# Half-empty key blocks of sliding-window attention multiplied as pairs of 128x64 array tiles

## The chip, the core and the metric

The kernel runs on one core of one Trainium2 chip. A core has five engines that run their own instruction streams and meet at semaphores: TensorE (PE, matrix multiply; its weight loads are listed apart as PEld), VectorE (DVE), ScalarE (ACT), GpSimd (POOL) and SyncE (SP, which here only issues DMAs). The metric is the device time of one execution in microseconds, as the median of the runs shown.

## The reference

The input is a sequence of 2048 tokens of 512 features. Four layers follow each other, linear attention (A), sliding-window attention (B), A, B, each on the layer-normalised input, each added to the residual. All have 32 heads of 16 features. Cut to what matters:

```python
def _A_ref(x, wqkv, wo):
    q, k, v = split(x @ wqkv)                       # 32 heads of 16
    phi = lambda t: jnp.where(t > 0, t + 1, jnp.exp(t)) + 1e-6
    pq, pk = phi(q), phi(k)
    kv = jnp.einsum("bhsd,bhse->bhde", pk, v)
    z = jnp.einsum("bhsd->bhd", pk)
    o = jnp.einsum("bhqd,bhde->bhqe", pq, kv) / (jnp.einsum("bhqd,bhd->bhq", pq, z)[..., None] + 1e-6)
    return merge(o) @ wo
...
def _B_ref(x, wqkv, wo):                            # window W = 256
    q, k, v = split(x @ wqkv)
    scores = jnp.einsum("bhqd,bhkd->bhqk", q, k) * (Dh ** -0.5)
    mask = (idx[:, None] - idx[None, :] >= 0) & (idx[:, None] - idx[None, :] < W)
    p = _softmax(jnp.where(mask[None, None], scores, -1e9), axis=-1)
    return merge(jnp.einsum("bhqk,bhkd->bhqd", p, v)) @ wo
...
x = x + _A_ref(_layernorm(x), A_wqkv, A_wo)
x = x + _B_ref(_layernorm(x), B_wqkv, B_wo)
x = x + _A_ref(_layernorm(x), A_wqkv, A_wo)
x = x + _B_ref(_layernorm(x), B_wqkv, B_wo)
```

## The kernel before, in words

The sequence is cut into 16 tiles of 128 tokens. The program runs in stages: the keys of layer 1 (`layer_a_keys`), a barrier in which the sums over all tokens become small matrices (`barrier`), then `middle(2)`, which for each tile ends layer 1, does all of layer 2 and begins layer 3, a second barrier, and `middle(3)`, which ends layer 3 and does layer 4. The two `middle` stages hold the sliding-window attention.

**Sliding window.** Two heads are worked on at once, so there are 16 pairs of heads, numbered by `f` (0 to 3) and `gq` (0 to 3). Keys stand in blocks of 64, and a block of two heads fills 128 partitions. For the key tile `j` (blocks 2j and 2j+1) `b_scores` multiplies the queries of the tiles j and j+1 with the keys in 32x128 array tiles, four `gq` at once (line 638), and ACT takes the exponential from PSUM into the buffer `pb` (line 648; in layer 4 a fourth buffer in `vp`). `b_far` does the same for the last 64 queries that a block reaches (lines 712 and 715, 725). Two triangles have to be cleared: the near one, on the diagonal (`mk`, lines 657 and 658, or 735 in layer 4), and the far one at the window's end (`mf`, lines 743 and 744). A mask is done on POOL by `affine_select` (657, 743) or on DVE by a product with a table of ones and zeros (658, 735, 744); which engine does which one is fixed by a table.

**Values.** `b_values(j, h)` is called for the query tile j and each half h, the pairs of heads with f = 2h and 2h+1. For each pair of heads it multiplies up to six key blocks, 128 probabilities columns of a block as the weights and the 34 value columns of the two heads (16 values and a one for each) as the moving side, into one PSUM bank (line 764). The six blocks of a tile are 2j, 2j-1, 2j-2, 2j-3, all of whose 128 columns matter, and two of which only half matters: of block 2j+1 only the last 64 queries see any key, and of block 2j-4 only the first 64. The other 64 columns of these two are zeros that stand in the buffer. A half thus takes 48 matmuls from the third tile on. Then DVE takes the reciprocal of the sums (`rcp`, line 775) and multiplies (`div`, line 776), a DMA transposes the result, and `b_out` projects it (line 406) and adds the residual (line 574). `b_values_end` does the last tile of layer 4 in another order.

**Order.** No loop order reaches the chip. `Plan` makes a list of operations with what each reads and writes. `place` takes from a packed table (`TABLE`) the place of every operation in one overall order, its engine where it has a choice, and its PSUM bank (8 banks). `synchronise` puts semaphore waits where an operation needs another engine's result. Each engine plays its operations in that order and waits in line: what stands behind a waiting instruction waits too. The costs in `act`, `dve`, `mm` and the like served to make the table and set nothing on the chip. `PAR` likewise.

Of the kernel before, what the change touches and what calls it, by code (L numbers as in the profile page):

```python
# [223 lines left out]
class Plan:  # L224
# [523 lines left out]

    def b_values(self, j, h, key):
        K = self  # L750
        rp = self.rp
        ps = Tile(1, K.cls)
# [3 lines left out]
        for f in (2 * h, 2 * h + 1):  # L756
# [16 lines left out]
        s = j % 2  # L773
        v = lambda: K.ps(ps)[:, 0:272].rearrange("p (u a d) -> p u a d", u=8, a=2)
        self.on("DVE", "rcp", lambda e: e.reciprocal(K.rc[:, s, h, :].rearrange("p (u a) -> p u a", a=2), v()[:, :, :, 16]), key + 0.02, dve(16, "recip"), wr=[("rc", s, h)], ps=[ps])
        self.on("DVE", "div", lambda e: e.tensor_tensor(
            K.o[:, s, :].rearrange("p (a r d) -> p r a d", a=2, d=DH)[:, 8 * h:8 * h + 8],
            v()[:, :, :, 0:16], K.rc[:, s, h, :].rearrange("p (u a) -> p u a", a=2).unsqueeze(3).to_broadcast([P, 8, 2, DH]), ALU.mult),
            key + 0.03, dve(256), rd=[("rc", s, h)], wr=[("o", s, h)], ps=[ps])

    def b_values_end(self, j, h, key):
# [22 lines left out]
        for k in range(2):  # L804
# [13 lines left out]
        s = j % 2  # L818
        v = lambda: K.ps(ps)[:, 0:272].rearrange("p (u a d) -> p u a d", u=8, a=2)
        self.on("DVE", "rcp", lambda e: e.reciprocal(K.rc[:, s, h, :].rearrange("p (u a) -> p u a", a=2), v()[:, :, :, 16]), key + 0.02, dve(16, "recip"), wr=[("rc", s, h)], ps=[ps])  # L820
        self.on("DVE", "div", lambda e: e.tensor_tensor(
            K.o[:, s, :].rearrange("p (a r d) -> p r a d", a=2, d=DH)[:, 8 * h:8 * h + 8],
            v()[:, :, :, 0:16], K.rc[:, s, h, :].rearrange("p (u a) -> p u a", a=2).unsqueeze(3).to_broadcast([P, 8, 2, DH]), ALU.mult),
            key + 0.03, dve(256), rd=[("rc", s, h)], wr=[("o", s, h)], ps=[ps])
# [44 lines left out]
    def middle(self, ph):  # L869
# [37 lines left out]
        for j in range(T):  # L907
# [12 lines left out]
            for h in range(2):  # L920
                (self.b_values_end if last and j == T - 1 else self.b_values)(j, h, base + j + (h + 1) / 2 + par["k_pv"])
# [26 lines left out]
    r"w;>IN#84O-U&1Rm4QcT;yn$122M8Gj73Rep@D}dEOo)f^F&*Z^{1^sj!8=HR=`jN~fWj~YhJr?e1+X9{#6;K-8o_&Tm>9!iI1G<fz+y(s3lT6P=7aoD05V}A",
    r"ER0343}nWl7#Xu*RxAa>ASp(|Bv>7bK}9Hr!=X54$C6kCDq&C<0okwwR>bmH11n%n3<R~X4(5c)SOp70Q*4IKu_{)>6|fRkK?|&njj=TbfwHg~nqW(;i}i2~",
    r"oPqk-5F20{JPVDm6_$W=a2|HSZrB5RVK|P!kvIy6;!K={v+)2P#Cz}oM&lS9i>q)S%)xQE8t39Lybt4X9?r*)Faa;XCs>0Eur0R3LpTK&;scn9YjGN`!x=ac",  # L950
    r"*W+%Sgza%MK7<a~1v}y%ED3vYDK5k1*a<h_BJ7MCaWO8z!&n*uQD6!}kDw}ih9fu~ui;U=j$hy+Uc$>*gl=FU42(r72p+@ZxB@rfJ-m;_Xg>zUV7M8#U}TCy",
    r"`|trqrLMRYA7M8PO2H^N6^CuO9dF_etOh6WBtF5F_!yt!Ej)#%@hYCdvsj!;&~1!HaVP|Zq;q(JPEvHbgYl>&ouar@m8#JdtWGf~7L}sXbQg!wa2i27@id*G",
    r"WH^#y(nCB;u_*y1$M}?pQebxsMWJaIj-t`@9zWnmEJNop3?-zpRE`o;N_>rP@Dq-qBvhV~QBn#^sqihn!*CRy(ozJfMYZW1UBL5HgT_)iN>3T60#&3+)QIX(",
    r"U7AiaXeKqG&-ewu;y3(`K=r65C8vyp)R;0+X39e2s6I8In?&>sFVHQzO<AcSF+IoeG=V143w(vms0B5ri*$)D(@QLcrLhc_#d6q^Qcy}tMcJr5b)b&aiRRE;",
    r"%1%v5NYOm1LTN~op&XQxQd2JKOc7~5Sz17gC=zv{uH<MT<)%Co1*2j#%uC&95>2Khw3s&1CYnOaC_2W#&9sGj;8I#at7tj(#9r7N``}7iP5CH46`)WYn!|8G",
    r"Dny0p5k00W6qdKrHrh_%_!T{&tF(h&Q+cky;W+}op?mazD$_N(PZhZm&!X<sgL+agx=U~ADfOm4)R%H#PHaWFupi~dJb06D@ojERvAGSkrH2%UBXVDyO>wy&",
    r"KBE`Zj;8Qb?oT^u7d@w!G>t3s8d^(LcsK2#z4V#B&@`G#Rk<2}rEj#3)>9Hr%HIhXIT`Px1RRN@G4Te9&M|lZ4WvXoh^BKwPRuFz4n^iDJcDQQEFMhNxi;6~",
    r"8<dKN&`^rXcQ_^A<usg*uTx!4&RKas9iW4BkF#-hPRmVsHZwP4VZ}MPIk)82yp%OB<5nD>4cFjzl%6fu<PQ{&m-8V?%{jRizo$>sf*l9qHk^xda~^KX?YRLr",
    r"<VJj-57QB9$499nf23aAn~%|P>cE}36UX9J+=u(}8qUl4I6trEIUJa~@H&pk{kT6D;DWrK3vpo%!W(!1H{lFCkQ;LmF3QDtEobBvJeN1}AYQ<kI16Xy{y2~4",
    r"^CsTR4|pLj;#d5d>+t{_f)6<;2jeX~5Z`cc9*l!<8*k@$vV-HxR!$%ZB?Rx};#`7Da(ynvr8$vw<-y#Ym+%lC%H4PvCzd4gl%Mf)4#|&r7eD4FJe)`HNZ!p!",  # L960
    r"Wj`O_gZ!EIaARpAhqx#A;1%+f_wguR%<uUNuav{wRGP^uIl|xgC?DewypliicLqU8Cg~-EB$rRzTv|v=*~=_SMsr44Eh1V{NJ<GJK_!c{lB|+VNP<alInF2e",
    r"B#+^-JdSfnE;+@g`3%41?2=P*O9%-m<9PzV<4_V>Qb_?RB&nsKyp?y7M)F8LIm_qxy}aO(Qc7A&ds!oS<vg#Iby8S9$VcfZy(N>BmNL>oUUEliBW<Ofgppp-",
    r"SNcn4xxo3Qtdx_m(oY765htG{oLuBfTwW^3dg&rvCA>tCh+^fle38q1g|G5Z877frr|go6+)XBNAc-u)rHJg7ic(2NNHK{bMJ2FI<_)q%ic24<EL9|(Y?XmB",
    r"NCwL|882yNo9vVQQdK5MCz&WiWTRA*O|n_8@pV2R)#V1)kVA4<qDnM5BGIL@)RgWrNhV7Pi6K)Yrks*9GF84xEIH`?(I$0Tv^pjy#3)uhq?R0&%W_4I%O0^R",
    r"unMYzsIyXA>c~mCE?4E6+>o2HSAwg$QcrG4eVHcHC8U}m-^8iVDukLTv*f#EQlMtbZON>%sIY2|%$0dEQo^VP(oh=7C>bqdB#^ozcjcbkm+)%41XB@IGZjuX",
    r"S1r^*wL>DRb8=n|slzIix*)M-ti+MH5?Mu2^JRf7ltuDD9!ezjNTRBX@<1(?C2~m~su(J!ilrW@+$yh%t>UP->alvFvMZ(XsC+7(dMwdYPIW{bRibjJ`0AKC",
    r"rB18->WnI&&Z=B$sVtM_5?vKkg;h~?PMudpR2fxP6;kb0NA*-aQ`uAp)mpVt<y3jqNflESR9jV1RZ^8z8BU-QszfTWN}`^tcIt)du6n8-Dyb^V<v5vosd}lb",
# [186 lines left out]
```

## Time and profile before

| | before |
|---|---|
| time, median of 3 runs (lowest to highest) | 407.0 us (405.63 to 408.3) |
| span of the profiled execution | 405.4 us, 18074 instructions |
| PE, PEld busy | 386.1 us (95%), 263.9 us (65%) |
| DVE, ACT, POOL busy | 333.6 us (82%), 341.5 us (84%), 149.2 us (37%) |
| granted TensorE clock | 1.000 |

The profiled execution's own time is given by its span alone, from the first to the last instruction: 405.4 us, 1.6 us under the median of the runs and just under the lowest. A busy PE counts each matmul until its result has drained, so matmuls overlap in it: "x48 ... 1.36" is 48 matmuls from the start of the first to the end of the last. In a row such as `L764 PE MATMUL ps<-vB,pb 128*128 128x34` the first pair is the shape of the array tile, rows and columns, and the second the moving operand. Idle time is listed with what ended it; idle time of an engine that nobody waits for costs nothing.

### The profile page before, as it was taken

What the parts mean: (1) busy time and instruction counts of PE and PEld (TensorE: products, weight loads), DVE (VectorE), ACT (ScalarE), POOL (GpSimd) and SP (SyncE); (2) the same over time, 40 slices, a digit from 0 to 9 for tenths busy, and PEclk for the clock granted to TensorE, in tenths of its full rate; (3) what the DMA queues carried; (4) which work ended last, traced back from release to release, by engine and by line L of the source; (5) the groups of instructions that cost most, each with busy time, mean ns of one, the idle gap of its engine ahead of it and who ended that gap; (6) DMA issues with size and microseconds to landing.
All of it is one profiled execution on the core that took longest, in us unless ns stands there. A gap on an engine that the chain in (4) does not pass through costs nothing.

```text
span 405.4 us, 18074 instructions
## 1 busy us (share of the span) xinstructions
PE 386.1 (95%) x7930; PEld 263.9 (65%) x8004; DVE 333.6 (82%) x759; ACT 341.5 (84%) x439; POOL 149.2 (37%) x243
## 2 busy tenths in 40 slices
PE   8999999998999999999999999999999999999896
PEld 3644776766576566666666777677767775566665
DVE  6998898979998798887858789997898759776775
ACT  2655568998999999999998445999999999999994
POOL 3555624534363545541752213141132221232212
PEclk9999999999999999999999999999999999999999
DMA  8734216333253545353232000335224433344443
GB/s 250 243 66 128 82 41 127 106 80 92 71 94 69 122 97 101 63 129 81 62 79 56 20 2 12 96 83 135 69 57 108 110 76 75 82 118 94 115 124 107
DMA packets 67062, 37.75 MB, mean 93 GB/s; under 512 B 47688, under 2 KB 62152, under 8 KB 66984
## 3 DMA queue, kind: packets, MB, share of 16 engines
q1 hardware_dynamic: 66640, 35.67, 36.3%
q8 instruction: 63, 1.03, 1.2%
q0 software_dynamic: 336, 0.92, 0.7%
q14 instruction: 15, 0.12, 0.1%
q10 hardware_dynamic: 8, 0.00, 0.0%
HBM read 6.29 MB, written 2.10 MB: 21 GB/s over the span
## 4 chain that ended last, share of the span: by engine, by line
PE 76%; ACT 16%; DVE 5%; issue 2%; DMA 1%; ACTq 0%
PE ps L406 25%; PE ps L420 19%; PE ps L764 13%; ACT pb L648 10%; PE ps L638 6%; PE ps L481 3%; PE ps L715 2%; ACT pb L725 2%; ACT vp L648 2%; PE ps L712 1%; DMA xT<-xn 1%; PE ps L1067 1%; ACT vp L725 1%; PE ps L457 1%; DVE XQ L563 1%
## 5 line engine op out<-in xcount | busy, mean ns | idle before, releaser
L648 ACT ACTIVATE pb<-ps 128x1024 bf16<-128x1024 f32 (+3 forms) x224 | 198.4, 974 | 7.1 <-PE ps L638 5.5
L764 PEld LDWEIGHTS ps<-vB,pb 128*128 128x128 bf16 x2496 | 75.2, 96 | 10.4 <-issue 3.9
L764 PE MATMUL ps<-vB,pb 128*128 128x34 bf16 x2496 | 80.2, 177 | 0.3 <-DVE pb L744 0.2
L420 PE MATMUL ps<-xT,wBp 128*128 128x128 bf16 x1024 | 68.5, 219 | 0.9 <-DMA xT<-xn 0.6
L420 PEld LDWEIGHTS ps<-xT,wBp 128*128 128x128 bf16 x1024 | 58.8, 98 | 10.9 <-issue 4.5
L429 ACT ACTIVATE tE<-ps 128x512 bf16<-128x512 f32 x64 | 37.6, 605 | 26.3 <-PE ps L406 16.5
L743 POOL TENSOR_SCALAR_AFFINE_SELECT pb<-pb 128x1024 bf16<-128x1024 bf16 x32 | 36.9, 1152 | 53.8 <-DVE pb L735 37.6
L657 POOL TENSOR_SCALAR_AFFINE_SELECT pb<-pb 128x512 bf16<-128x512 bf16 x51 | 34.3, 673 | 48.4 <-ACT pb L648 20.6
L725 ACT ACTIVATE pb<-ps 128x1024 bf16<-128x1024 f32 x50 | 49.3, 1052 | 2.0 <-PE ps L715 1.0
L574 DVE TENSOR_TENSOR xres<-ps,xres 128x512 bf16<-128x512 f32 x63 | 42.9, 682 | 9.4 <-PE ps L406 9.1
L370 POOL TENSOR_TENSOR rs<-ve,negh 128x1 f32<-128x1 f32 x64 | 37.2, 581 | 32.1 <-DVE ve L369 27.5
L638 PE MATMUL ps<-XQ,kB 32*128 32x256 bf16 (+3 forms) x992 | 47.0, 264 | 1.7 <-ACT pb L648 0.5
L406 PE MATMUL ps<-wA,XQ 128*128 128x512 bf16 x179 | 45.7, 379 | 1.8 <-issue 0.8
L367 DVE BATCH_NORM_STATS2 stats<-xres 128x6 f32<-128x512 bf16 x64 | 43.8, 686 | 2.7 <-DMA xres<-in_A_x_dram 1.8
L420 PE MATMUL ps<-XQ,wA 128*128 128x128 bf16 x512 | 35.4, 219 | 0.1
L369 POOL TENSOR_SCALAR ve<-mv 128x1 f32<-128x1 f32 x45 | 11.5, 255 | 64.4 <-DVE mv L368 62.4
L420 PEld LDWEIGHTS ps<-XQ,wA 128*128 128x128 bf16 x512 | 30.6, 98 | 5.5 <-issue 0.7
L406 PE MATMUL ps<-wBv,xT 128*128 128x512 bf16 x108 | 30.1, 380 | 2.9 <-issue 1.4
L638 PEld LDWEIGHTS ps<-XQ,kB 32*128 32x128 bf16 x992 | 14.9, 92 | 26.4 <-ACT pb L648 8.4
L406 PE MATMUL ps<-wBo,oT 128*128 128x512 bf16 x103 | 28.6, 380 | 3.1 <-issue 1.9
L406 PE MATMUL ps<-M,XQ 128*128 128x512 bf16 x114 | 29.7, 380 | 1.3 <-issue 0.6
L406 PEld LDWEIGHTS ps<-wA,XQ 128*128 128x128 bf16 x192 | 17.0, 97 | 19.6 <-issue 2.1
(128 smaller groups left out, 569.1 us busy)
## 6 DMA issues: line engine op xcount, KB each, us to landing
vB<-vS SPq DMA_DIRECT2D x64, 136.0 KB, 2.6
kB<-vp SPq DMA_DIRECT2D x64, 128.0 KB, 2.2
wA<-in_A_wqkv_dram SPq DMA_DIRECT2D x3, 512.0 KB, 5.0
out_dram<-xres SPq DMA_DIRECT2D x9, 128.0 KB, 2.8
xres<-in_A_x_dram SPq DMA_DIRECT2D x2, 512.0 KB, 4.9
pb<-in_B_wqkv_dram SPq DMA_DIRECT2D x1, 1024.0 KB, 5.6
out_dram<-xres POOLq DMA_DIRECT2D x7, 128.0 KB, 2.2
xres<-in_A_x_dram SPq DMA_DIRECT2D x3, 256.0 KB, 4.7
```

Source lines behind the costliest of these rows:

```text
L367: self.on("DVE", "stats", lambda e: e.bn_stats(K.stats[:, t, :], K.xres[:, t, :]), key, dve(512), rd=[("xres", t)], wr=[("stats", t)])
L370: self.pow = self.on("POOL", "pow", lambda e: e.tensor_tensor(K.rs[:, t, :], K.ve[:, t, :], K.negh[:], ALU.pow), key + 0.03, (640, 690), r ...
L406: m = e.matmul(K.ps(ps), lhs(c), rhs(c), start=c == 0, stop=c == 3)
L420: m = e.matmul(K.ps(ps)[:, f * P:(f + 1) * P], w(c, f), xT(c), start=c == 0, stop=c == 3)
L429: self.on("ACT", "E", lambda e: e.activation(K.tE[:, s, :], K.ps(ps), ACT.Exp, bias=0.0), key, act(512), wr=[("tE", s)], ps=[ps])
L574: self.on("DVE", "res", lambda e: e.tensor_tensor(K.xres[:, t, :], K.ps(po), K.xres[:, t, :], ALU.add), key, dve(512), rd=[("xres", t)], w ...
L638: m = e.matmul(K.ps(ps[gq])[:, ns * i:ns * i + ns], K.kB[rows, j % 4, 2 * f + b, :, :], K.XQ[rows, f, q:q + ns], start=True, stop=True, ti ...
L648: return e.activation(out(h, ns).rearrange("p (f g) c -> p f g c", f=n), i, ACT.Exp, bias=0.0, scale=0.25)
L657: return e.affine_select(out=x, in_=x, compare_op=ALU.is_ge, fill=0.0, base=1, pattern=[[0, 4 * n], [2, 64]], channel_multiplier=-1)
L725: return e.activation(o.rearrange("p (f g) b c -> p f g b c", g=2), i, ACT.Exp, bias=0.0, scale=0.25)
L743: return e.affine_select(out=x, in_=x, compare_op=ALU.is_ge, fill=0.0, base=-2, pattern=[[0, 16], [-2, 64]], channel_multiplier=1)
L764: m = e.matmul(K.ps(ps)[:, 34 * u:34 * u + 34], K.P((b // 2) % rp)[:, f, gq % 2 * 2 + gq // 2, o:o + P], K.vB[:, (b // 2) % 4, b % 2, r, : ...
```

## The change

For query tiles from the third on (but not the last of layer 4) `b_values` is replaced by `b_pairs`. It uses one PSUM bank for each half as before, and splits the 96 matmuls of a tile into two kinds of operation. Four operations, one for each `f`, hold the four full key blocks: 16 matmuls each on the whole 128x128 array. Two operations, one for each half, hold the two half-empty blocks: 16 matmuls with 64 weight columns each, those of block 2j-4 in the array's columns 0 to 63 and those of block 2j+1 in columns 64 to 127, one after the other, so that two neighbours work in different tiles of 128x64. They write PSUM partitions 0 to 63 and 64 to 127. The zeros are no longer read. The number of matmuls is the same: 864 of them (54 halves with 16) change from 128 to 64 weight columns. The four full operations no longer wait for the mask of the near triangle of block 2j+1 and that of the far triangle of block 2j-4; the small one does. `rcp` and `div` move into a helper, `divide`, unchanged.

The table is another one: the order, banks and engines of all operations are set anew. Beside the 54 new operations the engine differs for 114 others; in sum 13 masks go from POOL to DVE (7 of 128x1024, line 743 to 744, and 6 of 128x512, line 657 to 658), and some copies from PSUM go from DVE to ACT or back. In the program PE changes the shape of its array tiles 329 times before and 385 times now.

```diff
+    def b_pairs(self, j, key):
+        K = self
+        rp = self.rp
+        banks = [Tile(1, K.cls) for _ in range(2)]
...
+        full = ((2 * j, 0), (2 * j - 1, 64), (2 * j - 2, 128), (2 * j - 3, 192))
+        vals = lambda i: [("vB", i % 4, a, b) for a in range(2) for b in range(2)]
+        for f in range(4):
+            def put(e, f=f):
+                m = None
+                for gq in range(4):
+                    u = 4 * (f % 2) + gq
+                    for b, c in full:
+                        o = 384 * (b % 2) + c
+                        m = e.matmul(K.ps(banks[f // 2])[:, 34 * u:34 * u + 34], prob(b, f, gq)[:, o:o + P], val(b, f, gq), start=f % 2 == 0 and gq == 0 and b == 2 * j, stop=False, skip_group_check=True)
+                return m
+            rd = [("F", (j - 2) % rp, h_) for h_ in (0, 1)] + [("F", (j - 2) % rp, 1, 1)]
+            for i, bs in ((j - 2, (1,)), (j - 1, (0, 1)), (j, (0,))):
+                rd += [("P", i % rp, f)] + vals(i)
+                rd += [("P", i % rp, f, b, h_) for h_ in range(3) for b in bs]
+            self.pe("pv", put, key + 0.5 * (f // 2) - 0.001 * (f % 2), 16, 34, rd=rd, ps=[banks[f // 2]])
+        for h in range(2):
+            fs = (2 * h, 2 * h + 1)
+            def put(e, h=h, fs=fs):
+                m = None
+                for f in fs:
+                    for gq in range(4):
+                        u = 4 * (f % 2) + gq
+                        for half, b in ((0, 2 * j - 4), (1, 2 * j + 1)):
+                            o = 384 if half else 256
+                            m = e.matmul(K.ps(banks[h])[64 * half:64 * half + 64, 34 * u:34 * u + 34], prob(b, f, gq)[:, o:o + 64], val(b, f, gq), start=False, stop=True, tile_position=(0, 64 * half), skip_group_check=True)
+                return m
+            rd = [("F", (j - 2) % rp, h_) for h_ in (0, 1)] + [("F", (j - 2) % rp, 0, 1)] + vals(j - 2) + vals(j)
+            for f in fs:
+                rd += [("P", i % rp, f) for i in (j - 2, j)] + [("P", j % rp, f, 1, h_) for h_ in range(3)]
+            self.pe("pv", put, key + 0.5 * h, 16, 34, mode=(128, 64), occ=256, rd=rd, ps=[banks[h]])
+            self.divide(j, h, key + 0.5 * h, banks[h])
...
-            for h in range(2):
-                (self.b_values_end if last and j == T - 1 else self.b_values)(j, h, base + j + (h + 1) / 2 + par["k_pv"])
+            end = last and j == T - 1
+            if j >= 2 and not end:
+                self.b_pairs(j, base + j + 0.5 + par["k_pv"])
+            else:
+                for h in range(2):
+                    (self.b_values_end if end else self.b_values)(j, h, base + j + (h + 1) / 2 + par["k_pv"])
...
 TABLE = (
-    r"c-qx^1GFSt(r#$0ZQHhO+qP}nwr$(CZQHi_XPvtD&h*^wnSO8n_11b>mANZp2fp|sa-YnqbKl)_58WdNK!9-Dg#d<Npdb_oXow5(AUK4EFc2RSKtf0aiNU}f",
...
+    r"c-qBz1Jor~({Am;#u?kTZQIP)cE*#jZQIV+wrwM0BV+6D^PW4w+)R@1TmQPZ-|pVswRcrL^;C6rpY?`@Xg&gfun-QyLku56NC*WneQ|vWAR$D6L=X`oK~oTj",
...
```

On PE, near the end of layer 2's attention, this stood before (the first two rows are projections of the next layer; 764 the values; 638 the scores; a row's size is that of its output):

```order
L406 MATMUL ps<-wA,XQ 128x512 x4
L420 MATMUL ps<-XQ,wA 128x128 x16
L764 MATMUL ps<-vB,pb 128x34 x48
L638 MATMUL ps<-XQ,kB 128x256 x8
L764 MATMUL ps<-vB,pb 128x34 x48
L638 MATMUL ps<-XQ,kB 128x256 x8
L406 MATMUL ps<-wA,XQ 128x512 x8
L638 MATMUL ps<-XQ,kB 128x256 x8
```

At the same place there now stands (765 are the full key blocks, 783 the pairs, with 64 output partitions each):

```order
L406 MATMUL ps<-wA,XQ 128x512 x4
L420 MATMUL ps<-XQ,wA 128x128 x16
L765 MATMUL ps<-vB,pb 128x34 x32
L783 MATMUL ps<-vB,pb 64x34 x16
L638 MATMUL ps<-XQ,kB 128x256 x8
L765 MATMUL ps<-vB,pb 128x34 x32
L783 MATMUL ps<-vB,pb 64x34 x16
L638 MATMUL ps<-XQ,kB 128x256 x8
L406 MATMUL ps<-wA,XQ 128x512 x8
L638 MATMUL ps<-XQ,kB 128x256 x8
```

Nothing else moved here: each 48 became 32 and 16, and between the full blocks and the scores there is one more change of the array's shape.

On DVE, in the middle of layer 2, these rows stood from one residual sum (574) to the next; 367, 368 and 371 belong to a layer norm, 395 and 592 are copies from PSUM, 430 and 431 the feature map of layer 3, 658 a mask:

```order
L574 TENSOR_TENSOR xres<-ps,xres 128x512
L367 BN_STATS stats<-xres 128x6
L368 BN_AGGR mv<-stats 128x2
L371 TENSOR_SCALAR xn<-xres,mv,rs 128x512
L430 TENSOR_SCALAR tE<-tE 128x512
L431 SCALAR_TENSOR_TENSOR vp<-ps,tE 128x512
L395 CAST vS<-ps 128x32x16 x2
L658 TENSOR_TENSOR pb<-pb,tri 128x8x64
L371 TENSOR_SCALAR xn<-xres,mv,rs 128x512
L395 CAST vp<-ps 128x512
L658 TENSOR_TENSOR pb<-pb,tri 128x8x64
L574 TENSOR_TENSOR xres<-ps,xres 128x512
```

The same stretch now, with two of the large masks (744):

```order
L574 TENSOR_TENSOR xres<-ps,xres 128x512
L367 BN_STATS stats<-xres 128x6
L744 TENSOR_TENSOR pb<-pb,tri 128x16x64
L368 BN_AGGR mv<-stats 128x2
L430 TENSOR_SCALAR tE<-tE 128x512
L395 CAST vS<-ps 128x32x16
L431 SCALAR_TENSOR_TENSOR vp<-ps,tE 128x512
L395 CAST vp<-ps 128x512
L395 CAST vS<-ps 128x32x16
L371 TENSOR_SCALAR xn<-xres,mv,rs 128x512
L574 TENSOR_TENSOR xres<-ps,xres 128x512
L744 TENSOR_TENSOR pb<-pb,tri 128x16x64
```

Both far masks of one key tile, done on POOL before, have come into DVE's line, ahead of a copy that frees a PSUM bank; the near masks have gone to other places.

More of the change, by code (lines that the diff above doesn't have):

```diff
@@ L772, in b_values @@
             self.pe("pv", put, key - 0.001 * (f % 2), 4 * len(blocks), 34, rd=rd, ps=[ps])
[L773 to L779, printed above, removed]
+        self.divide(j, h, key, ps)
     def b_values_end(self, j, h, key):
@@ L817, in b_values_end @@
             self.pe("pv", put, key - 0.001 * (1 - k), 8, 34, rd=rd, ps=[ps])
[L818 to L824, printed above, removed]
+        self.divide(j, h, key, ps)
     def b_out(self, j, key, by_pe):
@@ L948 @@
[L948 to L967, printed above, removed]
```

98 lines of the change are left out of this document (65 added, 33 removed).

## The prediction, made before the changed kernel was run

> **What bounds the kernel now.** I read the page first, then the stages of the sliding window by stretches, then single places in PE's timeline. The page's busy times and its chain of waits:
>
> ```profile
> PE 386.1 (95%) x7930; PEld 263.9 (65%) x8004; DVE 333.6 (82%) x759; ACT 341.5 (84%) x439; POOL 149.2 (37%) x243
> ...
> PE 76%; ACT 16%; DVE 5%; issue 2%; DMA 1%; ACTq 0%
> PE ps L406 25%; PE ps L420 19%; PE ps L764 13%; ACT pb L648 10%; PE ps L638 6%; PE ps L481 3%; PE ps L715 2%; ACT pb L725 2%; ACT vp L648 2%; PE ps L712 1%; DMA xT<-xn 1%; PE ps L1067 1%; ACT vp L725 1%; PE ps L457 1%; DVE XQ L563 1%
> ```
>
> PE carries three quarters of the chain, the value matmuls (764) 13% of it, some 53 us. But ACT carries 16%. The busy times by stretch (columns: time, then PE, PEld, DVE, ACT, POOL, each with its count, clock, DMA share, GB/s), first the two sliding-window stages as a whole, then a stretch in each:
>
> ```profile
> 70.00:220.00 150.00, 143.92 (x3038) 96.84 (x3069) 126.53 (x283) 145.10 (x170) 69.45 (x105) 1.00 0.39 88
> 270.00:395.00 125.00, 118.45 (x3201) 85.02 (x3220) 96.94 (x223) 119.64 (x147) 32.55 (x39) 1.00 0.40 97
> ```
> ```profile
> 120.00:140.00 20.00, 18.39 (x422) 12.42 (x423) 16.17 (x39) 20.00 (x24) 9.61 (x16) 1.00 0.48 88
> 360.00:380.00 20.00, 18.66 (x527) 13.51 (x527) 13.25 (x33) 19.85 (x25) 5.55 (x8) 1.00 0.43 98
> ```
>
> Just where the change acts, ACT is busy 145.1 of 150 us and 119.6 of 125 us, without a pause in some stretches. PE and ACT are both nearly full there; over the 275 us ACT has 4.9 + 5.4 = 10.3 us to spare, and no shortening of PE can bring more than that.
>
> **What it removes.** PE's timeline near the end of layer 2's attention, the place whose order is shown above (start, length from first start to last end, then the instructions):
>
> ```profile
> 197.63 1.06 PE L420 MATMUL ps<-XQ,wA 128*128 128x128 bf16 x16
> 198.53 1.36 PE L764 MATMUL ps<-vB,pb 128*128 128x34 bf16 x48
> 199.82 0.40 PE L638 MATMUL ps<-XQ,kB 32*128 32x256 bf16 x8
> 200.15 1.36 PE L764 MATMUL ps<-vB,pb 128*128 128x34 bf16 x48
> ...
> 206.15 1.36 PE L764 MATMUL ps<-vB,pb 128*128 128x34 bf16 x48
> 207.44 0.34 PE L638 MATMUL ps<-XQ,kB 32*128 32x192 bf16 x8
> 207.72 1.07 PE L420 MATMUL ps<-XQ,wA 128*128 128x128 bf16 x16
> ```
> ```profile
> L764 PE MATMUL ps<-vB,pb 128*128 128x34 bf16 x2496 | 80.2, 177 | 0.3 <-DVE pb L744 0.2
> ```
>
> One value matmul lasts 0.177 us, 48 take 1.36: (1.36 - 0.177) / 47 = 0.025 us from start to start, for 34 columns. The 16 that become pairs are 16 x 0.025 = 0.40 us in each half.
>
> **What a pair costs.** The trace has no 128x64 tile. The nearest rows are the sums' 128x32 tiles (543), four side by side over the same 128 rows, and the far scores of layer 4 (715), 32x64 tiles, eight at once, two of them over the same rows:
>
> ```profile
> 44.80 0.40 PE L543 MATMUL ps<-XQ,zs 128*32 128x128 bf16 x16
> ```
> ```profile
> L543 PE MATMUL ps<-XQ,zs x128: 219/219/219, 44.8 to 306.2; 128*32 128x128 bf16 x128
> ```
> ```profile
> L715 PE MATMUL ps<-XQ,kB x896: 184/209/212, 259.7 to 382.3; 32*64 32x64 bf16 x180
> ```
> ```profile
> 365.49 0.33 PE L715 MATMUL ps<-XQ,kB 32*64 32x64 bf16 x32
> ```
> ```profile
> 365.49 0.71 PE L715 MATMUL ps<-XQ,kB 32*64 32x64 bf16 x64
> 366.13 1.07 PE L420 MATMUL ps<-xT,wBp 128*128 128x128 bf16 x16
> ```
>
> At 543, 16 matmuls have 0.40 - 0.22 = 0.18 us between first and last start: four rounds of four, three steps of 0.06. One 128-column matmul on the whole array takes as much ((1.06 - 0.22) / 15 = 0.056 in the first row above). So tiles beside each other, over the same rows, run at once. At 715 the first 32 start within 0.33 - 0.19 = 0.14 us, four rounds of eight in 0.035 each. In such a round every row of the array takes in two times 64 weight columns and two times 64 moving columns; a 128x64 pair takes in two times 64 and two times 34. So I expect no more than 0.035 a pair, and hardly less than the 0.025 of a single value matmul: eight rounds are 0.20 to 0.28 us. I take 0.25, near the 715 rows. The far ends: (0.71 - 0.21) / 63 = 0.008 a matmul over all 64, so 16 x 0.008 = 0.13 if only issue counts; and eight rounds of 8 x 0.008 = 0.064, 0.51, if the average round of 715 is what counts.
>
> [...]
>
> So PE saves 54 halves x (0.40 - 0.25) = 8.1 us (10.8 at 0.20, 6.5 at 0.28).
>
> **What it adds: changes of shape.** In the rows above, 48 value matmuls fill 48 x 0.025 = 1.21 us, but the scores start 1.29 after them: 0.08 for the change. Back: from 199.82 to 200.15 is 0.33. Eight score matmuls of 256 columns last 0.06 longer than eight of 192 (0.40 against 0.34), so two rounds of 256 stream for about 0.24, and 0.09 is left; at 207.44 it is 0.28 - 0.18 = 0.10. From 715 back to 420 the last start is at 365.49 + 0.71 - 0.21 = 365.99 and the next at 366.13, 0.14, of which 0.03 is its own. I take 0.09 (0.08 to 0.10). The order has 385 changes for 329: 56 x 0.09 = 5.0 us (4.5 to 5.6). PE's sum is 8.1 - 5.0 = 3.1 us less (0.9 to 6.3).
>
> **What it moves.** Masks and copies:
>
> ```profile
> L743 POOL TENSOR_SCALAR_AFFINE_SELECT pb<-pb 128x1024 bf16<-128x1024 bf16 x32 | 36.9, 1152 | 53.8 <-DVE pb L735 37.6 <-ACT pb L725 5.8 <-DVE vp L735 4.3
> L744 DVE TENSOR_TENSOR pb<-pb,tri 128x1024 bf16<-128x1024 bf16 x18 | 12.8, 713 | 0.1
> L658 DVE TENSOR_TENSOR pb<-pb,tri 128x512 bf16<-128x512 bf16 x17 | 7.6, 455 | 1.9 <-ACT pb L648 1.9
> L395 DVE CAST vS<-ps 128x512 bf16<-128x512 f32 x24 | 16.4, 688 | 3.8 <-PE ps L406 3.0 <-issue 0.8
> L395 ACT ACTIVATE XQ<-ps 128x512 bf16<-128x512 f32 x10 | 6.0, 604 | 1.0 <-PE ps L420 0.7
> ```
>
> DVE gets 7 x 0.713 + 6 x 0.455 = 7.7 us of masks and loses about one copy (net, 0.7): 7 us, on 126.5 of 150 and 96.9 of 125 us busy. That lies beside PE and ACT; if the cover went, it would cost all 7. A large mask is ready 0.44 us after its start sooner than on POOL. ACT keeps about its load in these stages (three copies of `bqe` go, three of `bve` and one of `bke` come, at 0.6 to 0.7 us); its other additions are clears in the first 60 us. At the start SP now issues the first `wA` load sixth instead of third, behind `x`:
>
> ```profile
> 1.72 0.50 SPq L286 DMA_DIRECT2D wA<-in_A_wqkv_dram  x1
> ...
> 8.27 1.89 PE L406 MATMUL ps<-wA,XQ 128*128 128x512 bf16 x8
> ```
> ```profile
> wA<-in_A_wqkv_dram SPq DMA_DIRECT2D x3, 512.0 KB, 5.0
> ```
>
> Three places of 0.5 us later it is issued at 3.2 and lands at 8.2, when the first product with it starts today: nothing, or half a microsecond.
>
> What the values wait for:
>
> ```profile
>   POOL pb L657: 1.0, 3
>   ACT pb L648: 0.9, 4
>   DVE pb L658: 0.8, 3
>   DVE pb L744: 0.7, 2
> ```
>
> Masks stop 764 for 1.0 + 0.8 + 0.7 = 2.5 us. Two of the four masks now bind only the small operation, so I count 1.0 us of this as gained, between 0 (it waits in turn, with the scores behind it in PE's line) and 2.5.
>
> **The rivals.** *A, the sum holds:* PE's 3.1 us count by its share of the chain, 76%, 2.4 us, plus 1.0. The span becomes 402.0. By the ends (0.9 and no wait, 6.3 and 1.0) it is 399.6 to 404.7.
>
> *B, the pairs do not pair:* each of the two tiles waits for the other's load, the small operation takes 16 x 0.025 = 0.40 us to 0.51, and the changes of shape are paid on top: 5.0 to 54 x 0.11 + 5.0 = 10.9 us, 76% of it 4 to 8 slower. It decides from a round of (0.40 - 5.0 / 54) / 8 = 0.038 us on, only just above my 0.035. Against it: 543 and the first rounds of 715. For it: 715's average of 0.064. [...]
>
> *C, ACT takes over:* with ACT at 97% and 96%, a PE that is 1% shorter only waits for PSUM banks. Nothing is gained, 405 to 407. The two full stretches are for it, the 10.3 us to spare against.
>
> *D, the new order as a whole is better:* PE stands still 150 - 143.9 + 125 - 118.5 = 12.6 us in the two stages. If half of it goes with the earlier full blocks and quicker masks, 6.3 + 2.4 = 8.7 us less, 398.
>
> *E, DVE's line is late:* all 7 us of it on the path and nothing gained: 414.
>
> **How the numbers follow.** The median of the runs is 1.6 us above this span, so A gives 402.0 + 1.6 = 403.6 (401.2 to 406.3). A measurement of this kernel tells 1%, 4.1 us, from no change. Chances: A 0.42, of which 0.16 under 402.9; B 0.13 (411 to 415); C 0.18; D 0.21 (396 to 401); E 0.06. Faster 0.16 + 0.21 = 0.37, within 1% 0.26 + 0.18 = 0.44, slower 0.19. The range from 396.5 to 411.5 leaves out most of B and E and the lowest of D.
>
> **What would show it.** The pair rows (783): 16 matmuls of 128x64 from first start to last end 0.25 + 0.18 = 0.43 us or less; over 0.58 is B. The start of what follows a pair, 0.08 to 0.10 after its last round, shows the change of shape. PE's busy time should fall by 3 to 8 us; if ACT's share of the two stages rises above 98%, it is C. Reciprocals (now 795) that wait for DVE's own masks would be E. The prediction fails if the rounds of 715 that I read come from instructions queued ahead and a pair behind 32 full matmuls finds none.

## The result, and the profile after

The changed kernel is slower: 411.4 us median of 6 runs (410.3 to 412.9) against 407.2 of 6 of before in the same measurement (405.6 to 408.3), a ratio of 1.0107 with an interval of 1.0080 to 1.0133. The profiled execution has a span of 410.1 us, 4.7 above before's 405.4.

The page's busy times and chain of waits, of after:

```profile
PE 383.8 (94%) x7928; PEld 259.3 (63%) x8004; DVE 337.2 (82%) x775; ACT 345.7 (84%) x442; POOL 136.1 (33%) x226
...
PE 68%; ACT 12%; DVE 10%; issue 4%; DMA 4%; POOL 1%; SPq 1%; POOLq 0%
```

PE's busy time fell by 2.3 us, and yet PE's share of the chain went from 76% to 68%: what grew are DVE (5% to 10%), DMA (1% to 4%) and issue (2% to 4%). The pairs themselves are just what was forecast. PE's timeline in layer 2 of after, at the same kind of place as shown of before:

```profile
209.53 0.96 PE L765 MATMUL ps<-vB,pb 128*128 128x34 bf16 x32
210.42 0.43 PE L783 MATMUL ps<-vB,pb 128*64 128x34 bf16 x16
210.78 0.34 PE L638 MATMUL ps<-XQ,kB 32*128 32x192 bf16 x8
211.06 1.07 PE L420 MATMUL ps<-XQ,wA 128*128 128x128 bf16 x16
```
```profile
L783 PE MATMUL ps<-vB,pb x768: 177/183/204, 94.6 to 400.7; 128*64 128x34 bf16 x192
```

From first to last start the 16 matmuls take 0.43 - 0.183 = 0.25 us, eight rounds of 0.031. The last of the 32 full matmuls starts at 209.53 + 0.96 - 0.177 = 210.31 and fills 0.025, so 0.08 is the change of shape; behind the pairs it is 210.78 - (210.42 + 0.25 + 0.03) = 0.08 again.

Where the time is lost is seen from when each stage's work starts first and last on PE. First the rows of before that the prediction does not show (the last start of layer 2's far scores, 712; first and last start of the scores, 638), then those of after, with the first barrier (543) and layer 4's far scores (715):

```profile
L712 PE MATMUL ps<-XQ,kB x448: 188/188/198, 86.0 to 217.2; 32*128 32x64 bf16 x150
L638 PE MATMUL ps<-XQ,kB x992: 188/265/278, 61.4 to 392.6; 32*128 32x256 bf16 x96, 32*128 32x224 bf16 x89, 32*128 32x192 bf16 x7, 32*128 32x128 bf16 x4
```
```profile
L543 PE MATMUL ps<-XQ,zs x128: 219/219/219, 48.2 to 308.7; 128*32 128x128 bf16 x128
L712 PE MATMUL ps<-XQ,kB x448: 185/188/198, 88.8 to 220.6; 32*128 32x64 bf16 x150
L715 PE MATMUL ps<-XQ,kB x896: 184/209/212, 263.0 to 385.8; 32*64 32x64 bf16 x180
L638 PE MATMUL ps<-XQ,kB x992: 188/265/278, 64.8 to 396.6; 32*128 32x256 bf16 x96, 32*128 32x224 bf16 x89, 32*128 32x192 bf16 x7, 32*128 32x128 bf16 x4
```

The first barrier starts at 48.2 instead of 44.8: 3.4 us are lost in a stage that has not one pair. From there the distance hardly moves: 3.4 at the first scores (64.8 against 61.4), 3.4 at the end of layer 2 (220.6 against 217.2), 3.5 at the last far scores of layer 4 (385.8 against 382.3). So up to there the two sliding-window layers, where all the pairs are, neither gained nor lost. The last scores are 4.0 late, and the end 4.7. Distances of half a microsecond mean little here: the kernel with pairs alone has the order of before up to the barrier, and its barrier starts at 44.3.

The first 45 us, by stretches (columns as before: PE, PEld, DVE, ACT, POOL), of before:

```profile
0.00:20.00 20.00, 18.65 (x135) 10.61 (x138) 15.44 (x44) 9.18 (x15) 9.10 (x26) 1.00 0.79 248
20.00:45.00 25.00, 24.84 (x218) 13.04 (x217) 22.31 (x56) 11.73 (x20) 14.79 (x32) 1.00 0.43 113
```

and of after:

```profile
0.00:20.00 20.00, 16.66 (x117) 8.69 (x119) 14.99 (x45) 8.33 (x15) 8.33 (x23) 1.00 0.77 236
20.00:45.00 25.00, 23.00 (x140) 11.68 (x142) 21.29 (x56) 12.33 (x19) 11.79 (x27) 1.00 0.60 123
```

PE, nearly full there before, is busy 2.0 + 1.8 us less in the same 45 us. SP's timeline of after (283 are loads of `x`, 286 and 291 of weights, 377 transposes), with DVE's first statistics and PE's first product:

```profile
0.80 2.43 SPq L283 DMA_DIRECT2D xres<-in_A_x_dram  x5
3.27 1.02 SPq L286 DMA_DIRECT2D wA<-in_A_wqkv_dram  x2
3.90 0.69 DVE L367 BATCH_NORM_STATS2 stats<-xres 128x6 f32<-128x512 bf16 x1 [2.71 <-DMA xres<-in_A_x_dram]
4.33 6.70 SPq L283 DMA_DIRECT2D xres<-in_A_x_dram  x2
8.70 0.59 PE L406 MATMUL ps<-wA,XQ 128*128 128x512 bf16 x2
11.08 0.51 SPq L286 DMA_DIRECT2D wA<-in_A_wqkv_dram  x1
13.04 1.29 SPq L377 DMA_TRANSPOSE XQ<-vp  x1
15.90 0.37 SPq L291 DMA_DIRECT2D wBo<-in_B_wo_dram  x1
16.32 0.51 SPq L286 DMA_DIRECT2D pb<-in_B_wqkv_dram  x1
20.06 5.18 SPq L377 DMA_TRANSPOSE XQ<-vp  x4
```

and of before:

```profile
2.86 1.46 DVE L367 BATCH_NORM_STATS2 stats<-xres 128x6 f32<-128x512 bf16 x2 [1.66 <-DMA xres<-in_A_x_dram]
7.50 0.37 SPq L286 DMA_DIRECT2D wA<-in_A_wqkv_dram  x1
11.27 0.37 SPq L286 DMA_DIRECT2D pb<-in_B_wqkv_dram  x1
16.37 6.01 SPq L377 DMA_TRANSPOSE XQ<-vp  x4
```

What SP waits for in the first 48 us, in after and in before:

```profile
SPq L283 <- DMA wA<-in_A_wqkv_dram: 5.7, 1, 5.7
```
```profile
SPq L283 <- DMA wA<-in_A_wqkv_dram: 1.1, 1, 1.1
```

With five loads of `x` issued at once, that of the tiles 2 and 3 ahead of that of the first tile, DVE starts at 3.90 instead of 2.86. The kernel's own rule for its loads (line 295) does the rest: from the eighth load of its list on, each waits until the load four places ahead in that list has landed. The last load of `x` therefore waits for the second `wA` load. That one is issued seventh now instead of sixth, and the waiting load stands ahead of the third `wA` load instead of behind it. SP stands for 5.7 us instead of 1.1, until 11.0, and the third `wA` load leaves at 11.08 instead of 7.50. The row of four transposes starts at 20.06 instead of 16.37.

### The profile page after: what moved, and what is told of

Same layout as the page of the kernel before. It is cut to its first block, busy times and chain, and to the rows that moved or that the text cites. A ratio compares the mean times of both kernels' runs of the same rounds, so it can differ in the third digit from the quotient of the medians.

```text
span 410.1 us, 18057 instructions
## 1 busy us (share of the span) xinstructions
PE 383.8 (94%) x7928; PEld 259.3 (63%) x8004; DVE 337.2 (82%) x775; ACT 345.7 (84%) x442; POOL 136.1 (33%) x226
## 4 chain that ended last, share of the span: by engine, by line
PE 68%; ACT 12%; DVE 10%; issue 4%; DMA 4%; POOL 1%; SPq 1%; POOLq 0%
PE ps L406 23%; PE ps L420 17%; PE ps L765 8%; PE ps L638 7%; ACT pb L648 6%; PE ps L783 4%; ACT pb L725 2%; DMA xres<-in_A_x_dram 2%; PE ps L481 2%; PE ps L715 2%; ACT vp L648 1%; DVE vp L431 1%; PE ps L712 1%; DVE stats L367 1%; DMA xT<-xn 1%
## 5 line engine op out<-in xcount | busy, mean ns | idle before, releaser
L429 ACT ACTIVATE tE<-ps 128x512 bf16<-128x512 f32 x64 | 38.2, 610 | 26.6 <-PE ps L406 20.4
L743 POOL TENSOR_SCALAR_AFFINE_SELECT pb<-pb 128x1024 bf16<-128x1024 bf16 x28 | 32.7, 1167 | 68.2 <-DVE pb L735 38.0
L765 PEld LDWEIGHTS ps<-vB,pb 128*128 128x128 bf16 x1536 | 48.2, 96 | 7.9 <-issue 2.6
L765 PE MATMUL ps<-vB,pb 128*128 128x34 bf16 x1536 | 52.1, 177 | 0.0
L406 PE MATMUL ps<-wA,XQ 128*128 128x512 bf16 x181 | 47.3, 379 | 3.8 <-DMA XQ<-vp 1.2
L657 POOL TENSOR_SCALAR_AFFINE_SELECT pb<-pb 128x512 bf16<-128x512 bf16 x45 | 30.8, 683 | 50.3 <-ACT pb L648 22.4
L638 PEld LDWEIGHTS ps<-XQ,kB 32*128 32x128 bf16 x992 | 15.0, 92 | 27.9 <-ACT pb L648 10.4
L795 DVE RECIPROCAL rc<-ps 128x16 f32<-128x16 f32 x64 | 16.3, 255 | 18.1 <-PE ps L783 15.7
```

Of the source, the lines that this page charges most:

```text
L406: m = e.matmul(K.ps(ps), lhs(c), rhs(c), start=c == 0, stop=c == 3)
L429: self.on("ACT", "E", lambda e: e.activation(K.tE[:, s, :], K.ps(ps), ACT.Exp, bias=0.0), key, act(512), wr=[("tE", s)], ps=[ps])
L638: m = e.matmul(K.ps(ps[gq])[:, ns * i:ns * i + ns], K.kB[rows, j % 4, 2 * f + b, :, :], K.XQ[rows, f, q:q + ns], start=True, stop=True, ti ...
L657: return e.affine_select(out=x, in_=x, compare_op=ALU.is_ge, fill=0.0, base=1, pattern=[[0, 4 * n], [2, 64]], channel_multiplier=-1)
L743: return e.affine_select(out=x, in_=x, compare_op=ALU.is_ge, fill=0.0, base=-2, pattern=[[0, 16], [-2, 64]], channel_multiplier=1)
L765: m = e.matmul(K.ps(banks[f // 2])[:, 34 * u:34 * u + 34], prob(b, f, gq)[:, o:o + P], val(b, f, gq), start=f % 2 == 0 and gq == 0 and b = ...
```

## The experiments

### The start, the order behind it, and the pairs

The change has three parts that can be exchanged: the first stage up to the barrier, the order (with engines and banks) behind it, and the pairs. Five kernels have them in other combinations.

Pairs alone, in the order of before:

```diff
-TABLE: order, engines and banks of the changed kernel
+TABLE: those of before; behind the full blocks of each half its 16 pairs
```

> Before's order, engines and banks; only the 54 value halves become 32 whole-array matmuls with the pair operation right behind. Theory 1 (the pairs do what PE's sum said, and the loss is from the new first stage): PE has about 3 us less to do, the time falls by 2 to 3 us, to about 404.5. Theory 2 (ACT or the banks set the pace of the two sliding-window stages, so a shorter PE only waits): within 0.5 us of before. Theory 3 (the changes of shape cost more than the pairs bring): 1 to 4 us slower than before.

408.9 us against 408.2, ratio 1.0008 (0.9985 to 1.0032). The pairs bring nothing that can be told from zero in the order of before; the interval leaves room for 0.6 us. There they need 397 changes of shape, so PE's own sum is 8.1 - 68 x 0.09 = 2.0 us less.

The new order without pairs:

```diff
-o = 384 if half else 256
-m = e.matmul(K.ps(banks[h])[64 * half:64 * half + 64, 34 * u:34 * u + 34], prob(b, f, gq)[:, o:o + 64], val(b, f, gq), start=False, stop=True, tile_position=(0, 64 * half), skip_group_check=True)
+o = 320 if half else 256
+m = e.matmul(K.ps(banks[h])[:, 34 * u:34 * u + 34], prob(b, f, gq)[:, o:o + P], val(b, f, gq), start=False, stop=half == 1, skip_group_check=True)
```

> The changed kernel with its order, engines and banks, but the half-empty blocks are again multiplied whole, with their zeros, on the 128x128 array; no 128x64 tile is left. Theory 1: PE has 3 us more than in the changed kernel, 413 to 414. Theory 2: as the changed kernel, 411 to 412. Theory 3: faster than the changed kernel, 408 to 410.

415.5 us, ratio 1.0156 (1.0118 to 1.0194), slower than any of the three theories had it.

The first stage exchanged, both ways (the first `den` is the barrier's first operation):

```diff
-TABLE: one kernel's order throughout
+TABLE: the other kernel's order, engines and banks up to the first den; its own behind
```

> The changed kernel with the order, engines and banks of before up to the first sums of the first barrier (the instructions on line 543), the loads from HBM included; from there on its own. Theory 1: the 3.4 us that the profile shows lost by then come back, 408.0. If the later stages take the gain up again (they wait for something that is not shifted with the start): 410 to 411.5.

> The kernel before with the first stage of the changed kernel (order, engines, banks up to the first barrier's sums) and its own order behind. Theory 1: 3.4 us slower, 410.5. If the loss at the start is made up later: 407 to 408.

The changed kernel with before's start takes 409.3 us, ratio 1.0018 (0.9995 to 1.0041); before with the new start 410.7, ratio 1.0070 (1.0042 to 1.0098). Last, before's start with the new order behind it, and no pairs:

> The changed kernel's order, banks and engines with the first stage of before, and the half-empty blocks multiplied whole, so without pairs. With the new first stage it was 1.0156. If start and pairs add up (0.9% and 0.5%): ratio 1.005 to 1.009, 409.5 to 411.5, and the order behind the start is itself 0.7% worse than before's. If the new order behind the start is as good as before's and the pairs bring nothing: 0.999 to 1.003. Below 0.998 the new order would be better and the pairs a loss.

410.5 us, ratio 1.0065 (1.0042 to 1.0088). All together:

| start | order behind it | half-empty blocks | ratio to before |
|---|---|---|---|
| before | before | pairs | 1.0008 |
| new | before | whole | 1.0070 |
| before | new | whole | 1.0065 |
| before | new | pairs | 1.0018 |
| new | new | whole | 1.0156 |
| new | new | pairs (the change) | 1.0107 |

The start costs 0.7 to 0.9% in each of the three lines where it can be compared (1.0070; 1.0156 against 1.0065; 1.0107 against 1.0018), 2.9 to 3.7 us. The new order behind it costs 0.65%, 2.6 us, by itself. The pairs bring 0.47% and 0.49% in the new order, 1.9 to 2.0 us (each with some 0.35 to 0.45% of uncertainty), and nothing in the old one. Taken in this sequence, order 2.6, start 3.7, pairs -2.0, the three make up the 4.3 us of the result, as they must: each is the difference of two lines of the table. What is found apart from that is that the start costs much the same in three lines, and the pairs in two.

### The loads at the start

```diff
-SP: x, x, x, x, x, wA, wA, x, x, wA
+SP: x, x, wA, x, x, wA, x, x, wA, x   (all ahead of the rest)
```

> The changed kernel; only the ten loads of x and of layer 1's weights on SP's queue stand in the order of before, ahead of all else. If the order of the loads makes the loss at the start: 3 us faster than the changed kernel, 408 to 409. If it is the order of the work on DVE, POOL and PE behind them: 410.5 to 412.

411.6 us against 408.8, ratio 1.0073 (1.0048 to 1.0098), where the changed kernel has 1.0107: a third of its loss, 1.4 us, though the two intervals overlap. Its microseconds lie in the second of the two ranges set ahead, but beside a before of 408.8; by its ratio it lies between the two. In the trace the first barrier starts at 46.2, between 44.8 and 48.2:

```profile
L543 PE MATMUL ps<-XQ,zs x128: 219/219/219, 46.2 to 307.1; 128*32 128x128 bf16 x128
```

So by this trace 2.0 of the 3.4 us are the order of the ten loads (1.4 by the runs), and the rest is that of the work behind them. The row of transposes belongs to the rest: with before's loads it still starts at 19.32.

### Whether PE or ACT sets the pace

The pairs save PE's time, yet bring nothing in the order of before. Four kernels take much from PE, from ACT, or from both, by leaving out parts of the computation. From ACT, the exponentials of the last 64 queries of most key tiles:

```diff
-i = span(ps[2 * h:2 * h + 2], lambda x: [[ns, n], x, [1, ns]])
+w = ns - 64 if j >= self.rp and ns > 160 else ns
+i = span(ps[2 * h:2 * h + 2], lambda x: [[ns, n], x, [1, w]])
```

and from PE, the half-empty key blocks:

```diff
+if j >= 2:
+    blocks = [(b, c) for b, c in blocks if b not in (2 * j + 1, 2 * j - 4)]
```

> The kernel before, but from the fourth key tile on (the fifth in layer 4) the exponential leaves out the last 64 of the 256 (224) queries that a block of scores holds; what the buffer held before stands there, so some probabilities are old. About 190 exponentials get 0.21 us shorter, 40 us off ACT. Theory 2 (ACT sets the pace of the two sliding-window stages): 8 us faster or more, until PE is the bound. If PE sets it: under 4 us faster.

> The kernel with the pairs alone in before's order, with the same part of the exponentials left out. Theory 2: with ACT out of the way the pairs now bring their 2 to 3 us against the same kernel without pairs. If the pairs bring nothing by themselves (their result is later, the masks hold them up): within 1 us of it.

> The kernel before without the two half-empty key blocks from the third tile on: 16 of 48 matmuls of a half are left out, with no change of shape, so 54 x 0.40 = 21.6 us are taken off PE (the result lacks these keys). If PE's time counts by its share of the chain, 76%: 391. Theory 2: a third of it or less, 400 or slower.

> Leaves out two parts of the computation: the two half-empty key blocks of each query tile (21.6 us off PE) and the exponentials of the last 64 queries of most key tiles (some 40 us off ACT). Alone the first was worth 2.9 us and the second 2.0. If PE and ACT hold each other (each nearly full, so that taking work from one leaves the other), both at once are worth far more than the 5 us of their sum: 12 us or more, 396 or less, ratio under 0.97. If instead a third thing sets the pace (DVE, transfers, the granted clock, the order itself), it stays at about the sum: 402 to 405, ratio 0.985 to 0.992. In the stretch 70:220 PE would be under 142 of 150 us in the second case and the stage would end more than 5 us sooner in the first.

All beside 408.8 us of before, the last beside 407.9:

| | us | ratio to before |
|---|---|---|
| exponentials cut (ACT's busy time falls by 31 us, not the 40 expected) | 406.5 | 0.9950 (0.9925 to 0.9974) |
| the same, with pairs | 405.3 | 0.9913 (0.9884 to 0.9942) |
| half-empty blocks dropped (PE: 864 matmuls x 0.025 = 21.6 us) | 405.6 | 0.9928 (0.9897 to 0.9958) |
| both dropped | 395.6 | 0.9688 (0.9647 to 0.9730) |

21.6 us off PE are worth 2.9 us, 31 off ACT 2.0, and both at once 12.7. By the marks set ahead, the first alone would have named ACT as the bound and the second alone PE. Neither is the bound by itself. That each holds the other is read from the chains and from one group of waits. The chain of waits with the half-empty blocks dropped, with the exponentials cut, and with both:

```profile
PE 53%; ACT 32%; DVE 9%; DMA 3%; issue 1%; SPq 0%; ACTq 0%
```
```profile
PE 88%; DVE 8%; ACT 2%; issue 1%; DMA 1%; POOL 0%; SPq 0%; ACTq 0%
```
```profile
PE 56%; DVE 22%; ACT 13%; DMA 5%; issue 3%; POOL 0%; DVEq 0%; POOLq 0%
```

With less on PE the chain passes to ACT (16% to 32%), with less on ACT to PE (76% to 88%), and with less on both to DVE (22%). The place of it is the scores. Their groups on PE (the last number is PE's idle time before them), of before and with the half-empty blocks dropped:

```profile
L638 PE MATMUL ps<-XQ,kB 32*128 32x256 bf16 (+3 forms) x992 | 47.0, 264 | 1.7 <-ACT pb L648 0.5
```
```profile
L638 PE MATMUL ps<-XQ,kB 32*128 32x256 bf16 (+3 forms) x992 | 47.4, 265 | 11.5 <-ACT pb L648 6.2
```

The scores need PSUM banks that ACT's exponential has to free. PE came there sooner and waited 11.5 us, 6.2 of it for that exponential, instead of 1.7. That the scores are the place is read from these rows; it was not tried apart. A part of what the dropped blocks save is lost to the clock: in 5 of its 8 runs the mean granted clock was 0.996 or less; its three others took 404.5 us in the mean, before's 17 of 24 at a higher clock 407.9, so that some 3.5 us are gained there (see the last section). The pairs, worth 2.0 us of PE's time in this order, gain 406.5 - 405.3 = 1.2 us where ACT has room, and nothing where it has not; the first of these differences (0.37% of ratio) is about as large as its own uncertainty.

### The last tiles

In the trace of the kernel with pairs alone, PE was 1.5 us ahead at the end of layer 2 (the last far scores at 215.7 instead of 217.2) and 1.5 behind at the last scores (394.1 instead of 392.6). Of the 1.5 ahead, 0.5 stood already at the first barrier, ahead of any pair.

```diff
-if j >= 2 and not end:
+if j >= 2 and not (last and j > 11):
```

> Pairs in the order, banks and engines of before, but the last three tiles with pairs in layer 4 keep their half-empty blocks whole: 48 pairs instead of 54. Pairs everywhere in this order gave 1.0008, up to 1.46 us ahead of before at the end of layer 2 and 1.5 behind at the end of the run, where PE waited and its granted clock then fell for 3.4 us. If that place is what loses the gain, this one keeps it: 405.5 to 407.5 against 408 of before, ratio 0.994 to 0.998, and no stretch of lower clock near 387. If the gain goes wherever PE is shortened beside a full ACT, it is 0.998 to 1.002 again.

408.3 us against 407.9, ratio 1.0006 (0.9981 to 1.0032): the last tiles are not what takes the gain away.

### Work moved between ACT, DVE and POOL

If a full ACT holds the pairs back, copies can be taken from it, onto a DVE that is 82% busy. And the masks that the change moves between POOL and DVE, which the prediction counted at nothing, can be exchanged by themselves.

```diff
-engine of 19 copies (10 in the second): ACT
+engine of these copies: DVE, at the same places in the order
```

> Pairs in the order and banks of before, and all 19 copies of queries, keys and values that ACT makes from the first scores on go to DVE instead, at their old places in the order: some 12 us off ACT (0.60 to 0.71 us each), some 13 us onto DVE (0.69 each). Nothing of the computation is left out. If PE and ACT hold each other and DVE has room (126 of 150 and 97 of 125 us busy), a third of what 40 us off ACT gave appears: 404.5 to 407 against 408 of before, ratio 0.992 to 0.998, ACT in 70:220 under 139 of 150 us. If DVE's line becomes the late one, as its place in the order is that of an ACT copy, the copies arrive late and PE waits: 409 to 414, ratio 1.003 to 1.015, with idle time of PE ended by DVE's copies.

> The same with every second one of these copies, 10 of 19: some 6 us off ACT, 7 us onto DVE. If PE and ACT hold each other and DVE has room, half of the gain of all 19: 406 to 408, ratio 0.995 to 1.0. If DVE's line is the late one: 408.5 to 411, ratio 1.001 to 1.008, and less than with all 19.

With 19 copies moved, 416.9 us against 407.2, ratio 1.0252 (1.0224 to 1.0281); with 10 of them 414.4, ratio 1.0182 (1.0153 to 1.0211). Both are beyond what was expected even of a late DVE: with some 12 us moved off a full ACT the kernel is 2.4% slower than with pairs alone. ACT's exponentials with pairs alone, and with all copies moved, in the stretch from 70 to 395 us:

```profile
L648 ACT ACTIVATE pb<-ps 128x1024 bf16<-128x1024 f32 (+2 forms) x216 | 191.4, 974 | 8.0 <-PE ps L638 6.7
```
```profile
L648 ACT ACTIVATE pb<-ps 128x1024 bf16<-128x1024 f32 (+3 forms) x208 | 185.3, 975 | 17.5 <-PE ps L638 16.2
```

ACT now waits 16.2 us for scores instead of 6.7, and the scores wait for DVE; the three longest waits of PE ahead of scores there are all on DVE, where with pairs alone one of 0.4 us was on DVE:

```profile
PE ps L638 <- DVE XQ L563: 1.7, 1, 1.7
PE ps L638 <- DVE vS L395: 1.0, 1, 1.0
PE ps L638 <- DVE XQ L395: 0.9, 1, 0.9
```

```diff
-engine of 51 masks: as in the kernel's own table
+engine of these masks: as in the other kernel (32 POOL to DVE and 19 DVE to POOL, or the reverse), same places
```

> Before, with every mask on the engine that the changed kernel uses for it, at its old place in the order: 32 masks go from POOL to DVE, 19 from DVE to POOL, 13 net as in the forecast. No other part of the change. If masks lie beside other work, as the forecast has it: 407 to 408.5, ratio 0.998 to 1.003. If DVE's line is one of those that hold the pace, as the 12 us of copies put on it showed (10 us slower), the 7.7 us of masks cost 3 to 8 us: 410 to 415, ratio 1.007 to 1.02.

> The changed kernel with the first stage of before (alone 1.0018), and behind it every mask on before's engine, at its new place in the order. If the new order was made for its own engines, this is slower: 410 to 414, ratio 1.004 to 1.015. If DVE's added masks cost time in the changed kernel too, it is faster than before: 404 to 407, ratio 0.99 to 0.998.

Before with the new masks takes 422.8 us against 407.4, ratio 1.0379 (1.0345 to 1.0412); the changed kernel with before's start and masks 418.9, ratio 1.0280 (1.0239 to 1.0320). Exchanged either way it costs 2.6 to 3.8%, more than was expected. In the second a part is the clock's: the mean granted clock was 0.986 to 0.992 in all six runs, and at the 0.990 of the trace that is an estimated 4 us of the 11.5 (1% of its 417.9). In the first, the last far scores of layer 2 start at 227.9 instead of 217.2. The longest waits of the values on PE, in the stretch from 70 to 250 us, are three for masks on POOL; the first two, at 181.2 and 219.7, are for masks that went there from DVE:

```profile
PE ps L764 <- POOL pb L657: 3.8, 3, 1.5
```

They are 2.7 of the 10.7 us; the rest was not followed. The exchange also sets other waits anew, as `place` lets the larger operations of POOL wait for the last large operation of DVE ahead of them, the masks among these. So this does not price the 13 masks of the change. It shows that an engine's choice belongs to its place in the order, and that neither can be costed alone.

## Why the prediction was wrong, point by point

**The pairs and the changes of shape: right.** 0.25 us for eight rounds and 0.08 for a change were measured where 0.25 and 0.09 were taken. Rival B, the pairs that don't pair, is out: a round takes 0.031, under its 0.038. A load of 64 columns lasts 0.113 us here (783), a matmul 0.183, and a round of two of each takes 0.031, so loads and matmuls of the two tiles overlap, though they share all rows. That each tile waits for the other's load, as B has it, is not what the trace shows of this tile. In the new order the pairs bring 55 changes of shape more than whole blocks do (385 against 330), so PE's sum of 3.1 us less stands. The sign that was set for it did not quite come: PE's busy time fell by 2.3 us, not by 3 to 8.

**PE counted by its 76% of the chain: right in size once, wrong as a rule.** 2.4 us were forecast; in the new order the pairs bring 1.9 to 2.0, in the old one nothing. So the near agreement is luck. A share of the chain is not an exchange rate: 21.6 us off PE brought 2.9 (13%), and once ACT was relieved too, 0.9688 instead of 0.9950, 10.7 us (half of it). Rival C, that ACT takes over, fits the old order with pairs, where nothing was gained, but it is not what decided the changed kernel.

**The mask waits, 1.0 us: not there to be gained.** The four waits that the prediction lists stand in an answer that takes PE's weight loads and matmuls together. Nearly all of them are the loads', which run ahead:

```profile
L764 PEld LDWEIGHTS ps<-vB,pb 128*128 128x128 bf16 x2496 | 75.2, 96 | 10.4 <-issue 3.9 <-POOL pb L657 1.0 <-ACT pb L648 0.9
```

The matmuls themselves waited for a mask once, for 0.2 us, as the prediction's own row of 764 on PE says (0.3 in all).

**The start: the first step that failed.** "Nothing, or half a microsecond" was worked out from the one `wA` load and the first product, and that product did come 0.4 us late (8.70 instead of 8.27). But what was moved were ten loads, and each tile's statistics, transposes and products come behind them in a stage where PE was full (43.5 of 45 us); it cost 2.9 to 3.7 us by the runs and 3.4 by the trace. The rest of SP's queue, in which a load of `x` now waits 5.7 us for a `wA` load, ahead of the third one, was not followed.

**The order as a whole: the second.** The sum had no term for it. Rival D gave it a gain of up to 6.3 us, and no rival gave it a loss of its own; E put a loss on DVE's masks alone. Measured without pairs and with before's start, it costs 0.65%, 2.6 us. D's 12.6 us in which PE stands still were also read too high: before's trace lacks 74 matmul records (7930 against 8004 weight loads), and 4.1 of the 12.6 are idle time that ended on no wait ("issue"), of which the trace of the changed kernel with before's loads, with all 8004 records, has none. What the order's loss consists of is not settled. In the trace of the kernel with before's start, the new order and no pairs (408.4, 3.0 over before) the barrier starts at 44.3, the last far scores of layer 2 at 217.6 and those of layer 4 at 383.8, where before has 44.8, 217.2 and 382.3: half of the loss comes behind the last far scores. DVE's two kinds of masks in after are

```profile
L744 DVE TENSOR_TENSOR pb<-pb,tri 128x1024 bf16<-128x1024 bf16 x22 | 14.9, 679 | 0.3 <-ACT pb L725 0.3
L658 DVE TENSOR_TENSOR pb<-pb,tri 128x512 bf16<-128x512 bf16 x23 | 9.8, 433 | 3.4 <-ACT pb L648 3.4
```

14.9 + 9.8 = 24.7 us where before had 12.8 + 7.6 = 20.4 (three more of the 13 stand in another buffer), and DVE's whole busy time grew by 3.6 us, not 7: half of E's 7 us were not there to be late. E's own sign, reciprocals that wait for DVE's masks, did not show: they wait for PE's pairs, 15.7 us, as they did for the values before, 15.9.

**The stages.** ACT is busy 144.6 and 120.3 us in the two stretches (145.1 and 119.6 before), so the mark set for C, above 98%, was not reached:

```profile
70.00:220.00 150.00, 142.37 (x2994) 94.26 (x3024) 126.88 (x286) 144.61 (x168) 64.57 (x98) 1.00 0.40 89
270.00:395.00 125.00, 117.27 (x3161) 83.16 (x3182) 98.78 (x229) 120.28 (x148) 28.51 (x38) 1.00 0.40 95
```

Of the forecast 403.6, then, -2.4 for the pairs held within half a microsecond in this order, -1.0 for the masks had no ground, and +3.7 for the start and +2.6 for the order were missing.

## What to carry to other kernels

When a change comes with a new order of everything, compare the stages that it does not aim at first: the first operation behind each stage, before and after, gives the loss of each in one row. Where two engines are both 95% full and free buffers for each other, as here, time taken from one was worth a small part of itself (2.9 of 21.6 us on PE, 2.0 of 31 on ACT), and only time taken from both brought more than the sum of these (12.7 us). A wait of a weight load is not a wait of PE: read it in the row of the matmuls (those of 764 in before stood idle for 0.3 us, its loads for 10.4). An engine's choice in an order laid out by hand or by search has no price of its own: moved at its old place, work that looks hidden can cost as much as it takes, or more. Here 10 copies, an expected 7 us for DVE, cost some 7, and the new masks in the order of before, by the forecast 7.7 us net for DVE, cost 15.4.

## What the runs showed of the hardware

The granted clock fell by half within a kernel whose PE was 82% busy in the 6 us ahead. In the kernel with half-empty blocks dropped, by stretches, 366 to 372 us and the 3.41 us behind it:

```profile
366.00:372.00 6.00, 4.95 (x163) 3.35 (x162) 4.26 (x10) 6.00 (x8) 1.25 (x2) 1.00 0.20 70
372.10:375.51 3.41, 3.41 (x40) 2.86 (x38) 1.51 (x3) 2.20 (x3) 0.43 (x1) 0.50 0.65 142
```
```profile
371.71 3.28 PE L420 MATMUL ps<-xT,wBp 128*128 128x128 bf16 x32
```

32 matmuls take 3.28 us there, where 16 take 1.06 at the full clock, and 32 would take 31 x 0.056 + 0.22 = 1.96. In the 6 us ahead PE's longest recorded wait was 0.5 us. The fall does not come in every run: in 95 runs of the kernel before, beside these experiments, the mean granted clock was 0.996 or less in 17, which took 410.1 us in the mean, and higher in 78, which took 407.6. With pairs alone it was so in 6 of 12 (409.6 against 408.1), with the half-empty blocks dropped in 5 of 8 (406.3 against 404.5), and in none of 18 runs with the exponentials cut and PE's work whole, or with pairs, where PE is busy nearly throughout (147.97 and 149.22 of the 150 us from 70 to 220). So in these three kernels the runs with a mean of 0.996 or less took some 1.5 to 2.5 us more. These counts would fit a PE that has less to do and waits more, but with 19 or 10 copies moved to DVE, where PE waits for DVE, none of 9 runs had such a mean. What sets it off is not shown.
